# Attention with soft-MoE slots: the order of the V products, a half chunk and a transposition within a pair of heads

## The chip, the cores and the metric

The kernel runs on one core of a Trainium2 chip. The metric is the device time of one execution in microseconds, as the median of several runs. In the profile PE is the matrix engine, PEld its weight loads, DVE the vector engine, ACT the scalar engine, POOL the general engine (it also issues the converting DMAs), SP the engine that issues plain DMAs.

## The reference

Eight images of 12 heads, 448 tokens, 64 channels go through attention whose softmax has one more term exp(-m) in its denominator. The result, as 3584 tokens of 768 channels, goes through a mixture of experts with 32 slots: slots gather tokens by a softmax over all tokens, eight experts of four slots each run two layers, tokens gather slots by a softmax over slots.

```python
scores = scale * np.matmul(q, k.transpose(0, 1, 3, 2))
m = np.max(scores, axis=-1, keepdims=True)
e = np.exp(scores - m)
attn = e / (np.sum(e, axis=-1, keepdims=True) + np.exp(-m) + 1e-09)
x = np.matmul(attn, v)               # then as [3584, 768]
logits = x @ phi                     # [3584, 32]
d = softmax of logits over the tokens;  c = softmax of logits over the slots
slot_input = d.T @ x                 # per expert e: 4 slots
slot_out[e] = np.maximum(slot_input[e] @ w1[e], 0.0) @ w2[e]
out = c @ slot_out
```

## The kernel before

**Pairs.** Heads are worked in 48 pairs (`NPAIR`), six pairs an image, three pairs a group. The 448 query rows of a head are three full chunks of 128 rows and a half chunk of 64; the half chunks of the two heads of a pair share 128 partitions. The loop over `s` is one pair step, its inner loop over `y` two half steps; `hs = 2*s+y`. The order in which the functions are called is the order on each engine (the schedule is written by hand), and an engine works strictly in that order.

**What a pair needs.**
- `T(n)`: 28 transpositions of q and k on PE into one PSUM bank, copied out by ACT (first pair of a group) or DVE (the two others), line 229.
- `A`, `A1`: scores with queries on partitions, only for the row maximum. A full chunk has two (line 268), each with a bank of `psA` and a DVE reduce of 0.6 us (line 270); the half chunk has one bank for both heads (lines 256, 259). They run some four pairs ahead, handed out from the list `runs`.
- `W1`, `W2`, `W3`: once a group, the maxima are negated (POOL), turned (PE) and copied (ACT), and exp(-m) is made (ACT).
- `AB(n, i)`: chunk i of pair n: scores with keys on partitions, minus the maximum by a second matmul (lines 354, 358), then ACT's exponential (line 360); around them the two maximum scores of a pair further on. `Bk(n, 3, 1)` is the half chunk.
- `AV(n, i, qs)`: V products from the exponentials, four key chunks i, into the one bank of `psV`; a column of ones in V gives the denominators. 24 matmuls of full query chunks and 8 of the half chunk (line 393).
- `N1`: the bank is copied to `ubuf` (ACT). `N2`: the denominators (two small DVE operations, lines 414 and 415) and the multiplications (three on POOL, lines 419 to 424).
- `PX(n)`: the pair's result is turned on PE (line 445) and copied to `xT` by ACT (line 451).
- `P(b)`: once an image, six steps for the MoE part, each hung to a half step in `post`: `l_mm` (logits, line 471), `l_turn`, `s_max`, `exps`, `s_mm` (slot inputs, line 539), `c_turn`. Each takes one `psA` bank, except `exps`.

**Banks.** `psA` has 3 (maximum scores, T, the chunk steps), `psB` 4 (scores, W2, PX), `psV` 1.

**Order of a pair step on PE before.** y=0: chunk 0, chunk 1, V products of the pair before (key chunks 2 and 3), a chunk step, their half-chunk products, N1. y=1: chunk 2, half chunk, T for pair s+6, W2, V products of this pair (key chunks 0 and 1), a chunk step, PX of pair s-2, N2.

**Weights and the end.** The first layer's weights and part of the second's are loaded by POOL's converting DMAs into `W` (11 places) during the pairs. Columns of the second layer of experts 4 to 7 come late into `R`, the place of the pairs' own tiles: the first half directly (`load_first`, by `col_at`), the second by way of `wd` in DRAM and SP's queue (`load_second`). After the last pair: `last` (the last image's steps), `hidden` (first layer, line 748), `slots` (second layer, line 764), `pick`, and the outputs, sent by SP as they are made.

Of the kernel before, what the change touches and what calls it, by code (L numbers as in the profile page):

```python
# [8 lines left out]
F32 = mybir.dt.float32  # L9
# [15 lines left out]
HG = 6  # L25
# [6 lines left out]
def kernel(  # L32
# [38 lines left out]
    ident2 = const.tile([128, 128], BF16, name="ident2")  # L71
# [7 lines left out]
    NQK, NE, VPN, NATV = 7, 5, HG * 4 * VS, HG * 4 * D  # L79
    sizes = [("nq0", 2 * NP * S), ("nq1", 2 * NP * S), ("nv", NATV), ("qk6", 2 * S), ("wm1", 512),  # L80
             ("qk0", 2 * S), ("qk1", 2 * S), ("qk2", 2 * S), ("wm0", 512), ("qk3", 2 * S), ("vp0", VPN),
             ("qk4", 2 * S), ("x0", 4 * DD), ("qk5", 2 * S), ("e2", NE * 2 * S), ("e1", S), ("vp1", VPN),
             ("xT", KC * 512), ("x1", 4 * DD)]
# [8 lines left out]
    e1_t = part("e1", 0, S)  # L92
# [3 lines left out]
    xT = part("xT", 0, KC * 512).rearrange("p (j s) -> p j s", j=KC)  # L96
# [23 lines left out]
    W = keep.tile([128, 11 * KC * F], BF16, name="W")  # L120
    w_tile = lambda i: W[:, i * KC * F:(i + 1) * KC * F]
# [10 lines left out]

    dram = ctx.enter_context(tc.tile_pool(name="dram", bufs=1, space=bass.MemoryType.DRAM))
    wd = [dram.tile([128, E2, ND], BF16, name=f"wd{z}") for z in range(FK)]

# [7 lines left out]
    with ExitStack() as at:  # L143
# [8 lines left out]
        ubuf = pu.tile([128, 2, 7 * W65], F32, name="ubuf")  # L152
# [27 lines left out]
        for h in range(2):  # L180
            nc.vector.tensor_add(ident2[:, 64 * h:64 * h + 64], ident[:, 0:64], ident[:, 64:128])
# [22 lines left out]
        mx, ngm, ec, mT, eT, av, us = {}, {}, {}, {}, {}, {}, {}  # L204
# [9 lines left out]
        def T(n):  # L214
            g, pl = divmod(n, NP)
            ps = psA.tile([128, 2, S], BF16, tag="a", name="ps_t")
# [20 lines left out]
        def A(n, i):  # L237
# [4 lines left out]
            if i < 3:  # L242
# [5 lines left out]
                for hl in range(2):  # L248
                    c = HG * i + 2 * pl + hl
                    nc.vector.reduce_max(mx[g][:, c:c + 1], pss[hl][:, 0:S], axis=AX.X)  # L250
            else:
# [6 lines left out]
                c = 3 * HG + pl  # L258
                nc.vector.reduce_max(mx[g][:, c:c + 1], ps[:, 0:S], axis=AX.X)  # L259

        def A1(n, i, hl):
# [7 lines left out]
            c = HG * i + 2 * pl + hl  # L269
# [3 lines left out]
        def W1(g):  # L273
# [4 lines left out]
            cols = lambda t: t[:, 0:3 * HG].rearrange("p (i c) -> p i c", i=3)[:, :, 2 * l0:2 * l1]  # L278
            o = w[:, 0:3, :].rearrange("p i (d c) -> p i d c", d=2)[:, :, :, 2 * l0:2 * l1]
            neg(o, cols(m).unsqueeze(2).to_broadcast([128, 3, 2, 2 * (l1 - l0)]))  # L280
            for hl in range(2):
                r = slice(64 - 64 * hl, 128 - 64 * hl)
                o = w[r, 3, :].rearrange("p (d c) -> p d c", d=2)[:, :, 2 * l0 + hl:2 * l1:2]
                neg(o, m[r, 3 * HG + l0:3 * HG + l1].unsqueeze(1).to_broadcast([64, 2, l1 - l0]))
            if l1 - l0 == NP:
                neg(nm, m)
            else:
                nc.gpsimd.memset(nm, 0.0)
                neg(cols(nm), cols(m))
                neg(nm[:, 3 * HG + l0:3 * HG + l1], m[:, 3 * HG + l0:3 * HG + l1])  # L290
            ngm[g] = nm

        def W2(g):
# [4 lines left out]
            nc.tensor.matmul(ps[:, 384:448], w[:, 3, :], ident2[:, 0:64], start=True, stop=True)  # L298
            st["ps_m"] = ps

        def W3(g):
# [3 lines left out]
            e = psm.tile([128, NP, 7], F32, tag="ec", name="ec", bufs=3)  # L305
            nc.scalar.activation(e[:, :, 0:6].rearrange("p l (i h) -> p i l h", i=3),
                                 ngm[g][:, 0:18].rearrange("p (i l h) -> p i l h", i=3, h=2),
                                 AF.Exp, scale=scale)
            nc.scalar.activation(e[:, :, 6], ngm[g][:, 18:21], AF.Exp, scale=scale)
            ec[g] = e  # L310


        def Bk(n, i, c=0):
# [11 lines left out]
            else:  # L325
# [3 lines left out]
                es = [e1_t]  # L329
# [69 lines left out]
        def N1(n):  # L399
# [4 lines left out]
            u = ubuf[:, n % 2, :].rearrange("p (s c) -> p s c", c=W65)  # L404
# [3 lines left out]
        def N2(n):  # L408
            g, pl = divmod(n, NP)
            b, pb = divmod(n, PB)  # L410
            u = us[n]
            eng = nc.gpsimd if on_pool(n) else nc.vector
# [474 lines left out]
```

## Time and profile before

| | |
|---|---|
| median of 3 runs | 312.85 us (311.38 to 315.28) |
| the profiled execution | 310.7 us, its span 308.9 us |
| PE, DVE, ACT, POOL busy, share of the span | 89%, 83%, 81%, 66% |
| pair steps 5 to 41 | 49.60 to 233.43 us |
| six pairs (186.14 to 216.00) | 29.86 us; DVE and ACT busy 28.56 and 28.57 |
| the first output transfer issued, the last landed | 278.8 us, 307.7 us |

A row of a group has the line, the engine, the operation, its tiles as out<-in with shapes and the count; then busy time and mean length of one in ns; then the engine's idle time just before, and what ended it. A row of the timeline has the start and the length in us, engine and line; a bracket gives the idle time before it and who ended that. A row of the windows has busy time and count for each engine, the granted clock of PE, and the DMA engines' share.

### The profile page before, as it was taken

The page shows a single profiled execution, that of the slowest core. Times are in us where ns is not written, and L with a number is a line of the kernel's source. Part 1 is how long each engine was busy: PE and PEld are TensorE (multiplying, and loading weights), DVE is VectorE, ACT ScalarE, POOL GpSimd, SP SyncE. Part 2 cuts the span into 40 slices and gives each one's busy share as a digit, 9 for nine tenths or more (in the row PEclk, how much of TensorE's full clock was granted, in tenths as well). Part 3 has the DMA queues.
Part 4 walks back from the last instruction along what each step waited for, and adds up shares of the span by engine and source line. Part 5 has one row for each costly group of instructions (what it writes and reads, how often), then busy time and mean ns, then how long its engine had stood idle before and what let it go on. Part 6 is the DMA issues. An engine that isn't in the chain of part 4 may idle for free.

```text
span 308.9 us, 12205 instructions
## 1 busy us (share of the span) xinstructions
PE 275.6 (89%) x5067; PEld 159.0 (51%) x5068; DVE 257.2 (83%) x607; ACT 249.3 (81%) x549; POOL 202.7 (66%) x403
## 2 busy tenths in 40 slices
PE   2899999999999999999999999999999899994810
PEld 1434456565666656665566566656665556451200
DVE  4778999999999999999999999999999566536930
ACT  2357599999999999999999999999999997236810
POOL 8682769788788878896889788879584863000000
PEclk9999999999999999999999999999999999999555
DMA  6999499999999999999999999999971999937997
GB/s 88 149 128 202 64 205 150 198 182 205 163 196 157 210 169 198 155 203 149 149 164 186 177 186 169 196 177 203 166 110 17 144 126 204 337 128 260 415 439 312
DMA packets 49350, 57.44 MB, mean 186 GB/s; under 512 B 2832, under 2 KB 41488, under 8 KB 48912
## 3 DMA queue, kind: packets, MB, share of 16 engines
q0 software_dynamic: 45536, 42.52, 90.1%
q1 hardware_dynamic: 3760, 14.16, 11.5%
q8 instruction: 39, 0.64, 0.8%
q14 instruction: 15, 0.12, 0.1%
HBM read 88.18 MB, written 14.16 MB: 331 GB/s over the span
## 4 chain that ended last, share of the span: by engine, by line
PE 50%; DVE 30%; ACT 7%; issue 4%; POOL 4%; DMA 1%; DVEq 0%; POOLq 0%
DVE mx L270 15%; PE ps_av L393 11%; PE ps_a L268 6%; PE ps_t L224 6%; PE ps_b L354 5%; PE ps_b L358 4%; DVE mx L250 3%; DVE mx L259 3%; PE ps_b L332 3%; PE ps_a L246 2%; DVE W L801 2%; DVE R L229 2%; PE ps_x L445 2%; ACT R L227 2%; PE ps_so L764 2%
## 5 line engine op out<-in xcount | busy, mean ns | idle before, releaser
L270 DVE TENSOR_REDUCE mx<-ps_a 128x1 f32<-128x448 f32 x248 | 136.6, 613 | 5.3 <-PE ps_a L268 5.1
L360 ACT ACTIVATE R<-ps_b 128x448 bf16<-128x448 f32 x272 | 131.0, 573 | 1.1 <-PE ps_b L358 0.8
L268 PE MATMUL ps_a<-R 64*128 64x448 bf16 x248 | 80.5, 352 | 1.8 <-DVE mx L270 1.8
L354 PE MATMUL ps_b<-R 64*128 64x448 bf16 x272 | 73.9, 353 | 0.9
L358 PE MATMUL ps_b<-mT,sel 64*128 64x448 bf16 x272 | 70.6, 350 | 0.0
L393 PEld LDWEIGHTS <-R 128*128 128x128 bf16 (+1 forms) x1536 | 50.5, 101 | 30.5 <-issue 26.4
L393 PE MATMUL ps_av<-R 128*128 128x65 bf16 (+1 forms) x1536 | 64.9, 196 | 0.1
L419 POOL TENSOR_TENSOR R<-ubuf,rec 128x384 bf16<-128x384 f32 x44 | 36.3, 825 | 37.9 <-DVE rec L415 23.4
L224 PEld LDWEIGHTS <-R 64*64 64x64 bf16 x1344 | 31.1, 113 | 19.2 <-issue 7.8
L338 ACT ACTIVATE R<-ps_b 128x448 bf16<-128x448 f32 x64 | 36.0, 579 | 5.9 <-PE ps_b L335 5.9
L224 PE MATMUL ps_t<-ident,R 64*64 64x64 bf16 x1344 | 32.0, 198 | 5.9 <-DMA R<-in_q_dram 4.3
L451 ACT CAST R<-ps_x 128x512 bf16<-128x512 f32 x47 | 28.1, 598 | 5.7 <-PE ps_x L445 5.7
L259 DVE TENSOR_REDUCE mx<-ps_a 128x1 f32<-128x448 f32 x48 | 29.6, 616 | 0.6 <-PE ps_a L256 0.3
L358 PEld LDWEIGHTS <-sel 64*128 64x128 bf16 x272 | 21.5, 94 | 14.9 <-issue 5.3
L268 PEld LDWEIGHTS <-R 64*128 64x128 bf16 x248 | 23.1, 94 | 9.8
L405 ACT COPY ubuf<-ps_av 128x455 f32<-128x455 f32 x44 | 25.2, 573 | 3.0 <-PE ps_av L393 2.8
L227 ACT COPY R<-ps_t 128x896 bf16<-128x896 bf16 x20 | 18.4, 922 | 11.3 <-PE ps_t L224 11.0
L250 DVE TENSOR_REDUCE mx<-ps_a 128x1 f32<-128x448 f32 x40 | 22.6, 618 | 4.3 <-PE ps_a L246 3.9
L332 PE MATMUL ps_b<-R 64*64 64x448 bf16 (+1 forms) x112 | 22.7, 386 | 0.0
L335 PE MATMUL ps_b<-mT,sel 64*64 64x448 bf16 (+1 forms) x112 | 21.5, 366 | 0.0
L424 POOL TENSOR_TENSOR R<-ubuf,rec 128x128 bf16<-128x128 f32 x44 | 17.5, 398 | 3.7
L354 PEld LDWEIGHTS <-R 64*128 64x128 bf16 x272 | 17.2, 94 | 4.7 <-issue 0.2
(132 smaller groups left out, 454.0 us busy)
## 6 DMA issues: line engine op xcount, KB each, us to landing
W<-in_moe_w_dram POOLq DMA_DIRECT2D x22, 768.0 KB, 9.5
R<-in_v_dram POOLq DMA_DIRECT2D x32, 192.0 KB, 4.6
out_dram<-W SPq DMA_DIRECT2D x2, 2688.0 KB, 10.3
R<-in_q_dram POOLq DMA_DIRECT2D x15, 336.0 KB, 7.4
R<-in_k_dram POOLq DMA_DIRECT2D x15, 336.0 KB, 8.5
wd<-in_moe_w_dram POOLq DMA_DIRECT2D x8, 384.0 KB, 10.0
R<-wd SPq DMA_DIRECT2D x8, 384.0 KB, 8.6
R<-in_moe_w_dram POOLq DMA_DIRECT2D x2, 768.0 KB, 8.3
```

The costliest lines, as they stand in the source:

```text
L224: nc.tensor.transpose(ps[r, a, c:c + 64], src[r, pl, tok * D:(tok + 1) * D], ident[r, r])
L250: nc.vector.reduce_max(mx[g][:, c:c + 1], pss[hl][:, 0:S], axis=AX.X)
L259: nc.vector.reduce_max(mx[g][:, c:c + 1], ps[:, 0:S], axis=AX.X)
L268: nc.tensor.matmul(ps[:, 0:S], t[r, 0, i * 128:(i + 1) * 128], t[r, 1, :], start=True, stop=True)
L270: nc.vector.reduce_max(mx[g][:, c:c + 1], ps[:, 0:S], axis=AX.X)
L332: nc.tensor.matmul(outs[hl], t[rs[hl], 1, cols], t[rs[hl], 0, :], start=True, stop=False)
L338: nc.scalar.activation(e, p[:, 0:S], AF.Exp, scale=scale)
L354: nc.tensor.matmul(ps[hl][:, 0:S], t[rs[hl], 1, cols], t[rs[hl], 0, :], start=True, stop=False)
L358: nc.tensor.matmul(ps[hl][:, 0:S], sel[rs[hl], h:h + 1].to_broadcast([64, 128]), mT[mg(n)][rs[hl], :], start=False, stop=True)
L360: nc.scalar.activation(e[:, hl, :], ps[hl][:, 0:S], AF.Exp, scale=scale)
L393: nc.tensor.matmul(o, eT[n, i, hl][:, qc], vp[g % 2][:, 2 * pl + hl, i, 0:W65], start=(i == 0 and u == 0 and hl == 0), stop=(i == 3), skip ...
L419: eng.tensor_mul(x[:, 0:3, c:c + 128].rearrange("p i (h d) -> p i h d", h=2), u[:, 0:6, 0:D].rearrange("p (i h) d -> p i h d", h=2), rec[: ...
```

## The change

- A pair step now is: y=0: chunk 0, half chunk, T for pair s+6. y=1: chunk 1, chunk 2, W2, the chunk step, PX of pair s-4, then all 32 V products of pair s-1, then N1. The list `runs` has the half chunk second, to match. The last four pair steps keep the old order; `px_at` hands out the PX left over.
- From pair 8 on, T writes to the bank of `psV` instead of one of `psA`.
- `N2` takes two pairs at once in every second pair step: one set of denominators (14 columns) and one small multiplication for both. The maxima's columns are sorted by pair for it, exp(-m) is one ACT operation and lives in one ring `ecr`; `ubuf` has four places for two, `e2` six for five, `e1` two for one.
- The chunk steps stand at odd half steps, one in each pair step, from `12*b + 21` on.
- `xT` has 448 columns an image slice for 512: PX turns the half chunk into 64 columns, `l_mm` takes it as two matmuls of 64 rows, `t_mm` reads it twice.
- The last two small operations of `c_turn` are done once for all images at the end.
- `W` is half a place smaller. The second half of expert 2's second layer goes to DRAM early (`w2d`) and by SP's queue into the place of expert 3's first layer once `hidden(0)` has read it. The first columns of expert 7 go to DRAM at s = 37 (`w3d`) and come by SP's queue, ahead of `load_second`.

```diff
-    NQK, NE, VPN, NATV = 7, 5, HG * 4 * VS, HG * 4 * D
+    NQK, NE, VPN, NATV = 7, 6, HG * 4 * VS, HG * 4 * D
...
-    W = keep.tile([128, 11 * KC * F], BF16, name="W")
+    NW = 21 * KC * F // 2
+    W = keep.tile([128, NW], BF16, name="W")
...
-        ubuf = pu.tile([128, 2, 7 * W65], F32, name="ubuf")
+        ubuf = pu.tile([128, 4, 7 * W65], F32, name="ubuf")
...
         def T(n):
             g, pl = divmod(n, NP)
-            ps = psA.tile([128, 2, S], BF16, tag="a", name="ps_t")
+            ps = (psA if n < 8 else psV).tile([128, 2, S], BF16, tag="a" if n < 8 else "v", name="ps_t")
...
-        def N2(n):
...
-            rec = psm.tile([128, 7], F32, tag="rec", name="rec", bufs=3)
-            nc.vector.scalar_tensor_tensor(rec, u[:, :, D], 1e-9, ec[mg(n)][:, pl, :], op0=ALU.add, op1=ALU.add)
+        def N2(*ns):
+            k, n0 = len(ns), ns[0]
...
+            nc.vector.scalar_tensor_tensor(rec, den, 1e-9, ecr[:, 7 * (n0 % 6):7 * (n0 % 6 + k)], op0=ALU.add, op1=ALU.add)
             nc.vector.reciprocal(rec, rec)
...
-                    for i in range(4):
+                    for i in range(3):
                         nc.tensor.matmul(v["ps_l"][:, i, :], xT[:, j, i * 128:(i + 1) * 128], phi_sb[:, j, :],
                                          start=(j == 0 and i == 0), stop=(j == KC - 1), skip_group_check=True)
+                for j in js:
+                    for r in (slice(0, 64), slice(64, 128)):
+                        nc.tensor.matmul(v["ps_l"][r, 3, :], xT[:, j, 384:S], phi_sb[:, j, :],
+                                         start=False, stop=(j == KC - 1), skip_group_check=True)
...
-                nc.vector.tensor_scalar(r, r, 1e-9, None, op0=ALU.add)
-                nc.vector.reciprocal(r, r)
...
-                post[2 * (PB * b + PB + 2) + z + (z > 2) + (z > 4) if b < B - 2 else 2 * (PB * b + PB + 2) - 1 + z] = f
+                hs = 2 * (PB * b + PB + 4) + 1
+                post[hs + 2 * z - (max(z - 2, 0) if b == B - 3 else 0) if b < B - 2 else hs - 3 + z] = f
...
-        runs = [(n, i) for n in range(NPAIR) for i in range(4)]
+        runs = [(n, i) for n in range(NPAIR) for i in (0, 3, 1, 2)]
...
+        px_at = {88: (40,), 89: (41,), 92: (42,), 93: (43, 44), 95: (45,)}
...
-                elif s < NPAIR:
+                elif s == 2 or s >= NPAIR - 4:
                     AB(s, 2 * y)
...
+                elif y == 0:
+                    AB(s, 0)
+                    Bk(s, 3, 1)
+                    if s < NPAIR - 6:
+                        T(s + 6)
+                else:
+                    AB(s, 1)
+                    AB(s, 2)
...
+                    elif s % 2 and s >= 3:
+                        N2(s - 3, s - 2)
...
+                if hs in post:
+                    post[hs]()
...
+                if y and not tail:
+                    if s < NPAIR - 5 and s >= 4:
+                        PX(s - 4)
+                    if s:
+                        for i in range(4):
+                            AV(s - 1, i, range(3))
+                        for i in range(4):
+                            AV(s - 1, i, [3])
+                        N1(s - 1)
...
         AV(n, 3, range(4))
+        nc.sync.dma_start(out=late[0][:, 3, :, :], in_=w3d)
         load_second(0, 4)
...
         hidden(0, h0, range(2))
+        nc.sync.dma_start(out=w_two, in_=w2d)
         last[3]()
+        nc.vector.tensor_scalar(crec, crec, 1e-9, None, op0=ALU.add)
+        nc.vector.reciprocal(crec, crec)
```

## The prediction

> **What bounds the kernel now.** I read the page first, then the busy times of one six-pair round, then the groups by line, then the timeline of a pair, last the end of the kernel.
>
> ```profile
> span 308.9 us, 12205 instructions
> PE 275.6 (89%) x5067; PEld 159.0 (51%) x5068; DVE 257.2 (83%) x607; ACT 249.3 (81%) x549; POOL 202.7 (66%) x403
> ...
> PEclk9999999999999999999999999999999999999555
> ```
>
> ```profile
> core 0: us, PE busy (x) PEld busy (x) DVE busy (x) ACT busy (x) POOL busy (x), PEclk, DMA share, GB/s
> 186.14:216.00 29.86, 29.35 (x593) 18.24 (x591) 28.56 (x68) 28.57 (x65) 25.45 (x50) 1.00 1.18 186
> ```
>
> ```profile
> L270 DVE TENSOR_REDUCE mx<-ps_a 128x1 f32<-128x448 f32 x248 | 136.6, 613 | 5.3 <-PE ps_a L268 5.1
> ...
> L229 DVE COPY R<-ps_t 128x896 bf16<-128x896 bf16 x28 | 17.2, 615 | 0.0
> ```
>
> The page has PE, DVE and ACT near each other and the clock full until the last three slices. The window 186.14 to 216.00 is six pairs (one round: the work repeats every six, 12 heads making one image), 4.98 us a pair. DVE and ACT are both busy 28.56 of 29.86 us. PE's 29.35 is no demand: a matmul row lasts 0.35 us though the next starts 0.19 us later, so short waits hide in it. The timeline of one pair shows them.
>
> ```profile
> 204.54 3.23 DVE L270 TENSOR_REDUCE mx<-ps_a 128x1 f32<-128x448 f32 x6
> 205.17 0.35 PE L268 MATMUL ps_a<-R 64*128 64x448 bf16 x1 [0.30 <-DVE mx L270]
> 205.45 0.79 PE L393 MATMUL ps_av<-R 128*128 128x65 bf16 x20
> 206.17 0.36 PE L268 MATMUL ps_a<-R 64*128 64x448 bf16 x1
> ...
> 206.56 0.35 PE L268 MATMUL ps_a<-R 64*128 64x448 bf16 x1
> 206.84 0.38 PE L332 MATMUL ps_b<-R 64*64 64x448 bf16 x2
> ...
> 207.29 0.63 PE L224 MATMUL ps_t<-ident,R 64*64 64x64 bf16 x28
> ...
> 207.85 0.54 PE L393 MATMUL ps_av<-R 128*128 128x65 bf16 x12
> ...
> 208.23 0.39 PE L445 MATMUL ps_x<-ident,R 128*128 128x128 bf16 x4
> ...
> 208.55 0.36 PE L268 MATMUL ps_a<-R 64*128 64x448 bf16 x1
> ...
> 208.95 0.62 DVE L270 TENSOR_REDUCE mx<-ps_a 128x1 f32<-128x448 f32 x1 [0.33 <-PE ps_a L268]
> ```
>
> Six reduces take 3.23 us: one each 0.53. PE's score matmul at 205.17 waited for the first of them (ended near 205.11): a `psA` bank is free again 0.06 us after its reduce. An idle DVE starts 0.40 us after the matmul (208.55, 208.95). So the loop is: PE fills three `psA` banks, DVE empties them at 0.53 us, and PE may be away from scores only as long as these banks feed DVE. Now the V products are away for 0.7 us (20 of them) and 0.4 us (12), and DVE hardly idles: 1.3 us per round. PE's own starts, added up without these waits, make some 28.4 us a round, so DVE sets the pace, with PE close behind.
>
> **The change, steady pairs (s = 5 to 41).** They run from 49.60 (first score of pair step 5) to 233.43, 183.8 us.
>
> Savings by rows: the two denominator operations take 0.31 us from start to start (L414, L415), once for two pairs: 0.15 a pair off DVE. `c_turn` loses L548 and L549, 0.3 a round. One mode change of PE less a pair, 0.1. ACT: one of two exponentials of 0.2 us in three pairs, and 64 of 512 columns of a 598 ns copy (0.05 to 0.07). DVE's demand falls from 28.56 to about 27.4 a round. That is the whole gain on offer, 1.2 a round.
>
> The price is the order. After the change PE does in a pair: chunk 0, half chunk, T, chunk 1, chunk 2, PX, all 32 V products. DVE does: two reduces, half chunk's reduce, T's copy, (every second pair) the denominators, then the four reduces of chunks 1 and 2. Intervals by the rows above: chunk's first to second score 0.39, into the half chunk 0.28, to T 0.45, T and mode change 0.56, chunks 1 and 2 0.97 (0.39+0.19+0.39). The last score is thus due at 2.65 us. Its bank is the one of chunk 1's first score, three allocations earlier, so it also needs DVE at: 0.40 + 3 x 0.53 + 0.58 + 0.06 = 2.63; plus 0.53 where DVE copies T (two pairs of three); plus 0.30 with denominators. From that last score to the next pair's first: 0.28 into PX, 0.19 for PX, 0.72 for the first 20 V products and 0.37 for 12 more, 1.56 us (plus 0.21 where W2 stands there, each third pair). At its start DVE has three reduces left, 1.5 us of work, and gets the next 1.56+0.40 later: half a microsecond idle in every pair, which is new.
>
> Pairs by s modulo 6, without chunk steps of the MoE part: 0: 2.65+1.56 = 4.21; 1: 5.04; 2: 4.95; 3: 4.51; 4: 4.74; 5: 5.25. Sum 28.7.
>
> The chunk steps (`P(b)`) now all stand between the last score and PX, where PE alone sets the time; before, they lay in PE's slack. A step's own `psA` tile waits for chunk 1's second reduce, about 0.55 after the last score where PE is there at 0.28 (with W2 at 0.49). So: l_mm 0.27 + 0.88 (18 full matmuls at 0.025, 12 halves, two mode changes of 0.1); l_turn 0.06 + 0.2; s_max 0.27 + 0.06; s_mm 0.06 + 0.7 (28 at 0.025); c_turn 0.27 + 0.06. Together 2.8 a round; their DVE work is hidden there. 28.7 + 2.8 = 31.5 a round, 5.25 a pair, against 29.9 now. Over 37 pairs: six rounds 189.0, the last pair 5.5 (with its l_turn), less 1.7 for steps 5 to 9, where no image is complete yet: 192.8 against 183.8, **+9.0 us**. Bounds: if the steps' matmuls found cover (28.7 a round) it would be -6; if the half microsecond were idle on top of today's 1.3 a round, +17.
>
> No cost taken: T into `psV` needs the copy N1 of the block before (ACT, done about 0.65 into the pair; T is due at 1.12), and the V block needs T's copy (at 2.6 by DVE, 2.8 by ACT; due at 3.1). If that cover of 0.3 to 0.5 were gone it would cost about 0.5 a pair. POOL's two pairs of multiplications (L419, 825 ns, and L424) come once for two pairs; PX is a pair later than that, some 5 us of cover. What queues behind them on POOL are the loads, none of them due sooner than two pairs. A fourth `ubuf`, a sixth `e2`, and the earlier T on loaded q and k: nothing waits.
>
> **The change, from s = 42 on.** s = 42 and 43 take 4.5 and 5.8 against 4.46 and 5.03: +0.8 (s_mm and 12 V products more in s = 43). The last four pairs go by ACT (4.00 of 4.00 busy from 244 to 248), and get two more PX copies (0.45 each) and l_ev: **+1.1** (0 to 2). Then the new transfer `w_two`:
>
> ```profile
> 258.92 7.67 SPq L141 DMA_DIRECT2D R<-wd  x8
> ...
> 268.75 1.48 PE L748 MATMUL ps_h<-W,ubuf 128*32 128x512 bf16 x24
> ...
> 272.44 0.34 PE L764 MATMUL ps_so<-W 128*32 128x384 bf16 x3
> ```
>
> ```profile
> out_dram<-W SPq DMA_DIRECT2D x2, 768.0 KB, 4.3
> ```
>
> It may start when hidden(0) has read its place, about 268.6 (before the row at 268.75), stands on SP's queue behind nine other transfers, and is wanted half way through the slots that start at 272.44, at 273.1. A transfer of 768 KB took 4.3 us, so 272.9 at best plus issue; behind the others, whose last landed at 274.7 now (some 2 us sooner, as 768 KB of converting loads leave the busy stretch), 274 to 276. I take **+1** (0 to 3): the output transfers start only after it, so all of it reaches the end. The two operations on `crec` moved here lie under 7 us of matmuls: 0. Of DMA rings the Trainium skill says that descriptors are consumed in ring order on each engine (DMA: Bandwidth & Descriptors, Queues, rings and completion order); by it `w_two` gets nothing before the nine, near the middle of that range, and by the 4.3 us row alone it would cost 0.
>
> Sum: 9.0 + 0.8 + 1.1 + 1 = +11.9. The profiled execution took 310.7 us (308.9 span), so 322.6; the median shown is 312.85, 2.15 above it, so 324.75, and I say **324**. A measurement of this kernel tells about 2% from no change: 306.6 to 319.1.
>
> **Rivals.**
> - Faster: the three-bank ring never runs dry, because T's tile has left `psA` (eight tiles a pair before, seven now). Then DVE works without idling: 27.4 a round, -2.5 x 6.2 = -15, +2.9 after: 300.6. It decides from the point where PE's way from last to first score falls under DVE's remaining 1.5 us less 0.4. For it: DVE is near saturated today, and a block costs one mode change less. Against: 1.56 is longer than 1.1, by rows. 0.13.
> - No change: half of the steps' matmuls and half of the idle time find cover; a round stays near 30: 313 to 317. For it: a PE wait hidden in 0.35 us rows can be shorter than I think. 0.18.
> - Worse: the one `psV` bank passes between T, its copy, the block and N1, and one of the four is late each time by 0.5: 37 x 0.5 more, 342. Against: cover above. 0.06.
> - Much worse: PE's clock. PE will stand up to 0.8 us in most pairs; should the granted clock fall to the 0.5 that the page shows in its last three slices (from 286 us), the streamed part (some 3.7 us a pair) doubles and a pair takes about 8.5: 37 x 3.3, near 430. The trace speaks against it: the wait at 205.17 is of this kind and PEclk is 1.00 in the whole round. 0.01. The Trainium skill describes such a failure, micro-idle gaps between matmul groups that let the clock oscillate (TensorE: Matmul & The Clock Gate, A second HAM failure mode); this trace has not shown it.
>
> **How the numbers follow.** Forecast (318 to 331) 0.62; no change 0.18; faster 0.13; worse or much worse 0.07. Range: the forecast's own with the upper half of the rivals below it, 309 to 332. Faster 0.13, same 0.18, slower 0.69.
>
> **What would show it.** Right: in a pair after the change, DVE idle about 0.5 us before the first reduce, ended by PE's first score; PE waiting 0.5 to 0.8 us before the last score, ended by DVE's reduce; a round of 31 to 32 us; DVE's busy time in it near 27.4; PEclk 1.00. PE idle before the second half of the first slots, ended by the DMA of `w2d`. Wrong: a round under 30 us, DVE busy above 95%, or T waiting for ACT's N1.

## The result and the profile after

The changed kernel took 327.47 us (median of 4 runs, 326.98 to 329.55), the kernel before 312.12 us beside it. The ratio is 1.0486 with a 95% interval of 1.0396 to 1.0576: slower by about 15 us. The forecast was 324 in a range of 309 to 332.

The page of the changed kernel, its first lines and the granted clock:

```profile
span 325.7 us, 12324 instructions
...
PE 274.5 (84%) x5115; PEld 162.3 (50%) x5116; DVE 249.1 (76%) x548; ACT 249.0 (76%) x532; POOL 193.7 (59%) x394
...
PEclk9999999999999999999999999999999999998555
```

Before, PE, DVE and ACT were busy for 89%, 83% and 81% of the span, now for 84%, 76% and 76%. DVE did get less work, 249.1 us against 257.2. But no engine is full any more, and the span is 16.8 us longer. So the added time is waiting. The groups by line say who waits (the last field is the idle time before the row's instructions, and who ended it):

```profile
L289 DVE TENSOR_REDUCE mx<-ps_a 128x1 f32<-128x448 f32 x248 | 137.9, 612 | 25.7 <-PE ps_b L366 10.3
...
L287 PE MATMUL ps_a<-R 64*128 64x448 bf16 x248 | 81.1, 352 | 13.1 <-DVE mx L289 12.1
```

The row of the score matmuls in the kernel before:

```profile
L268 PE MATMUL ps_a<-R 64*128 64x448 bf16 x248 | 80.5, 352 | 1.8 <-DVE mx L270 1.8
```

DVE's reduces waited for 5.3 us before and wait for 25.7 now. PE's score matmuls waited for 1.8 us before and wait for 13.1 now, nearly all of it for DVE. Each of the two engines waits for the other, at different places of the pair. The list of waits gives the count and the longest of one:

```profile
PE ps_a L287 <- DVE mx L289: 12.1, 26, 0.6
...
DVE mx L289 <- PE ps_b L366: 10.3, 14, 1.5
```

All of DVE's 25.7 us stand before the first reduce of a pair, 0.40 or 0.47 us after the pair's first score. (The profile names the instruction that ended last before the reduce could start, so some of these waits stand under line 366, the score matmul next to line 287 on PE.) In the steady pairs s mod 6 = 0 to 5 they are 0.62, 0.34, 0.49, 0.56, 0.38 and 1.05 us long. PE's waits for DVE stand before the last score of a pair in four pairs of six, 0.60, 0.34, 0.28 and 0.65 us for s mod 6 = 1, 2, 4 and 5.

The timeline of one pair (the second of six, step s with s mod 6 = 1, without an image's chunk step of PE) shows both waits in place:

```profile
216.18 0.36 PE L287 MATMUL ps_a<-R 64*128 64x448 bf16 x1
...
216.58 1.16 DVE L289 TENSOR_REDUCE mx<-ps_a 128x1 f32<-128x448 f32 x2 [0.34 <-PE ps_a L287]
...
217.25 0.60 PE L243 MATMUL ps_t<-ident,R 64*64 64x64 bf16 x28
...
218.18 0.61 DVE L248 COPY R<-ps_t 128x896 bf16<-128x896 bf16 x1
...
218.71 0.18 DVE L428 SCALAR_TENSOR_TENSOR rec<-ubuf,ecr 128x14 f32<-128x14 f32 x1
...
218.92 0.24 DVE L429 RECIPROCAL rec<-rec 128x14 f32<-128x14 f32 x1
...
219.08 2.15 DVE L289 TENSOR_REDUCE mx<-ps_a 128x1 f32<-128x448 f32 x4
...
219.69 0.35 PE L287 MATMUL ps_a<-R 64*128 64x448 bf16 x1 [0.60 <-DVE mx L289]
219.97 0.37 PE L463 MATMUL ps_x<-ident,R 128*128 128x128 bf16 x4
```

From the same timeline, the lines that follow:

```profile
221.25 0.36 PE L287 MATMUL ps_a<-R 64*128 64x448 bf16 x1
...
221.72 1.16 DVE L289 TENSOR_REDUCE mx<-ps_a 128x1 f32<-128x448 f32 x2 [0.49 <-PE ps_a L287]
```

PE's last score of the pair (219.69) waited 0.60 us for a `psA` bank, because DVE began the four reduces of chunks 1 and 2 at 219.08 only, behind the copy of T and the denominators. Then PE is away from scores for 1.56 us, until 221.25. DVE runs dry meanwhile and waits 0.49 us for the next pair's first score. The order makes the pair 219.69 − 216.18 + 1.56 = 5.07 us long. One round of six pairs, from the windows:

```profile
190.55:222.19 31.64, 29.17 (x603) 18.61 (x599) 27.72 (x61) 28.57 (x64) 24.22 (x49) 1.00 1.15 179
```

The round takes 31.64 us for 29.86, with DVE busy for 27.72 of it (28.56 before) and the clock of PE at 1.00.

Where the span grew, stage by stage, from the times of the first instruction of each stage in the two traces:

| stage | before | after | difference | forecast |
|---|---|---|---|---|
| start to the first score of step 5 | 49.60 | 48.48 | −1.1 | 0 |
| steps 5 to 41 | 183.8 | 194.7 | +10.9 | +9.0 |
| steps 42 and 43 | 9.49 | 10.96 | +1.5 | +0.8 |
| step 44 to the last image's logits | 17.52 | 19.59 | +2.1 | +1.1 |
| from there to `slots` | 12.01 | 12.03 | 0 | 0 |
| `slots` to the first output transfer | 6.35 | 8.35 | +2.0 | +1 |
| first output issued to last landed | 28.92 | 30.44 | +1.5 | 0 |

The differences add up to 16.9 for 16.8 us of span.

### The profile page after: what moved, and what is told of

Its sections match the earlier page's. It is cut to its first block, busy times and chain, and to the rows that moved or that the text cites. A ratio compares the mean times of both kernels' runs of the same rounds, so it can differ in the third digit from the quotient of the medians.

```text
span 325.7 us, 12324 instructions
## 1 busy us (share of the span) xinstructions
PE 274.5 (84%) x5115; PEld 162.3 (50%) x5116; DVE 249.1 (76%) x548; ACT 249.0 (76%) x532; POOL 193.7 (59%) x394
## 4 chain that ended last, share of the span: by engine, by line
PE 42%; DVE 38%; POOL 6%; issue 4%; DMA 3%; ACT 3%; DVEq 0%; POOLq 0%; ACTq 0%
DVE mx L289 20%; PE ps_av L405 14%; PE ps_a L287 6%; DVE mx L278 6%; DVE R L248 4%; PE ps_x L463 3%; DVE mx L269 3%; DMA W<-w2d 2%; PE ps_o L843 2%; PE ps_t L243 2%; PE ps_b L366 2%; PE ps_s L562 2%; PE ps_so L811 2%; DVE rec L429 1%; PE ps_l L489 1%
## 5 line engine op out<-in xcount | busy, mean ns | idle before, releaser
L289 DVE TENSOR_REDUCE mx<-ps_a 128x1 f32<-128x448 f32 x248 | 137.9, 612 | 25.7 <-PE ps_b L366 10.3
L372 ACT ACTIVATE R<-ps_b 128x448 bf16<-128x448 f32 x272 | 130.1, 565 | 8.3 <-PE ps_b L370 7.5
L287 PE MATMUL ps_a<-R 64*128 64x448 bf16 x248 | 81.1, 352 | 13.1 <-DVE mx L289 12.1
L405 PE MATMUL ps_av<-R 128*128 128x65 bf16 (+1 forms) x1536 | 56.0, 195 | 1.2 <-DVE R L248 0.7
L405 PEld LDWEIGHTS <-R 128*128 128x128 bf16 (+1 forms) x1536 | 48.6, 100 | 7.4 <-issue 4.6
L243 PEld LDWEIGHTS <-R 64*64 64x64 bf16 x1344 | 30.1, 112 | 16.0 <-issue 5.4
L350 ACT ACTIVATE R<-ps_b 128x448 bf16<-128x448 f32 x64 | 34.9, 564 | 4.0 <-PE ps_b L347 3.8
L243 PE MATMUL ps_t<-ident,R 64*64 64x64 bf16 x1344 | 30.6, 195 | 5.5 <-DMA R<-in_q_dram 4.2
L417 ACT COPY ubuf<-ps_av 128x455 f32<-128x455 f32 x44 | 24.5, 557 | 12.1 <-PE ps_av L405 12.0
L370 PEld LDWEIGHTS <-sel 64*128 64x128 bf16 x272 | 24.7, 95 | 13.0 <-issue 2.1
L469 ACT CAST R<-ps_x 128x448 bf16<-128x448 f32 x47 | 26.3, 564 | 2.0 <-PE ps_x L463 1.8
L287 PEld LDWEIGHTS <-R 64*128 64x128 bf16 x248 | 23.2, 94 | 8.2 <-issue 0.9
L246 ACT COPY R<-ps_t 128x896 bf16<-128x896 bf16 x20 | 18.4, 918 | 10.9 <-PE ps_t L243 10.8
L296 POOL TENSOR_SCALAR R<-mx 128x18 bf16<-128x18 f32 (+5 forms) x68 | 16.8, 253 | 12.5 <-DVE mx L269 6.4
L463 PEld LDWEIGHTS <-R 128*128 128x128 bf16 x192 | 12.6, 99 | 12.7 <-issue 11.1
```

The costliest lines, as they stand in the source:

```text
L243: nc.tensor.transpose(ps[r, a, c:c + 64], src[r, pl, tok * D:(tok + 1) * D], ident[r, r])
L287: nc.tensor.matmul(ps[:, 0:S], t[r, 0, i * 128:(i + 1) * 128], t[r, 1, :], start=True, stop=True)
L350: nc.scalar.activation(e, p[:, 0:S], AF.Exp, scale=scale)
L370: nc.tensor.matmul(ps[hl][:, 0:S], sel[rs[hl], h:h + 1].to_broadcast([64, 128]), mT[mg(n)][rs[hl], :], start=False, stop=True)
L372: nc.scalar.activation(e[:, hl, :], ps[hl][:, 0:S], AF.Exp, scale=scale)
L405: nc.tensor.matmul(o, eT[n, i, hl][:, qc], vp[g % 2][:, 2 * pl + hl, i, 0:W65], start=(i == 0 and u == 0 and hl == 0), stop=(i == 3), skip ...
```

## The experiments

The main theory: the order of the pair costs the time, since PE is away from scores longer than three banks feed DVE, and DVE has the copy of T and the denominators ahead of the reduces that PE waits for. The rivals: the one `psV` bank now shared by T; the mode changes of PE (scores run as 64*128, the V products and PX as 128*128; the first matmul of the other form starts 0.28 us after a score, as at 219.97 above, where a further score starts after 0.19) and the new half-chunk forms; the chunk steps that lost their cover; the late second-layer transfer. Ratios are against the kernel before. Plain differences are of medians, against the changed kernel where nothing else is said.

### The new transfer put first in its queue

```diff
-        load_second(4, 8)
...
         nc.sync.dma_start(out=w_two, in_=w2d)
+        load_second(4, 8)
```

> The changed kernel with one edit: the last four transfers of load_second are issued behind w_two instead of ahead of it. Theory (the 2.0 us for which PE stands still in the first slots come from w_two lying behind eight transfers on SP's queue): w_two lands 2 to 3 us earlier, the slots' row shrinks from 3.16 to about 1.2 us, and the whole kernel is 2.0 us shorter (1.5 to 2.3), near 325.4. Rival (the transfer is late because it cannot start before hidden(0) is done): the wait stays above 1.5 us and the time within 0.5 of 327.5.

Measured: 325.62 us, 1.0464 (1.0423 to 1.0505), 1.85 less than the changed kernel. The end of the changed kernel, in its timeline:

```profile
281.38 0.32 SPq L819 DMA_DIRECT2D W<-w2d  x1
...
285.77 0.34 PE L811 MATMUL ps_so<-W 128*32 128x384 bf16 x3
...
288.44 0.32 PE L811 MATMUL ps_so<-W 128*32 128x384 bf16 x1 [1.67 <-DMA W<-w2d]
```

And the row of that transfer in the list of DMA issues (size, time from issue to landing), first of the changed kernel, then of the experiment:

```profile
W<-w2d SPq DMA_DIRECT2D x1, 768.0 KB, 7.0
```

```profile
W<-w2d SPq DMA_DIRECT2D x1, 768.0 KB, 4.3
```

PE stood 1.67 us for the transfer, which took 7.0 us behind the others and takes 4.3 us ahead of them. It was issued at about the same time in both (281.38, 281.62). The `slots` stage is back at 6.35 us. So the two microseconds come from the place in the queue, not from the transfer itself. The Trainium skill says that descriptors are consumed in ring order on each engine (DMA: Bandwidth & Descriptors, Queues, rings and completion order); these two rows agree with it.

### The denominators behind chunk 2

```diff
-                    elif s % 2 and s >= 3:
-                        N2(s - 3, s - 2)
                 else:
+                    if s % 2 and s >= 3 and not tail:
+                        N2(s - 3, s - 2)
```

> The changed kernel with one edit: N2 of two pairs stands behind chunk 2 (where DVE idles during the V products) instead of behind T. Theory (PE's last score waits for the reduce of chunk 1's first score, and whatever DVE does ahead of that reduce lengthens the pair): pair steps 1, 3 and 5 of six lose 0.3 us each, 0.9 a round, 5 to 5.5 us in all, near 322. Rival (DVE's total work or PE's alone sets the pace, the place of two small operations is indifferent): within 1 us of 327.5.

Measured: 324.42 us, 1.0432 (1.0389 to 1.0475), 3.05 less, where 5 to 5.5 less was expected. The three odd pairs of a round (s mod 6 = 1, 3, 5) became 0.31, 0.22 and 0.30 us shorter, as they should. But the pair with s mod 6 = 2 became 0.56 longer (6.32), and a round is only 0.2 us shorter. So steps 5 to 41 have no more than 1.2 of the 3.05 us; 1.1 stand behind the pairs, where the edit changes no order (`slots` to the first output 7.63 for 8.35, the output phase 30.01 for 30.44). The list of waits of this run has a row that was not foreseen:

```profile
PEld L312 <- POOL R L296: 8.6, 8, 1.4
```

Line 312 is `W2` on PE, line 296 `W1` on POOL. `W1` now stands on POOL behind the multiplications of two pairs, which began half a step later.

### The same, with the negated maxima ahead of the multiplications

```diff
-                    if s % 2 and s >= 3 and not tail:
+                    if s % 2 and s >= 3 and s % 3 != 1 and not tail:
                         N2(s - 3, s - 2)
...
                     W1((s + 2) // 3 + 1)
+                if s % 2 and 3 <= s < NPAIR - 4:
+                    N2(s - 3, s - 2)
```

(The added call stands under `if s % 3 == 1`, so that each pair of pairs is still worked once.)

> e2_denoms_late with N2 called behind W1 where both fall into one pair step (s = 1 modulo 6). Theory (in e2_denoms_late W1 stands on POOL behind the multiplications of two pairs, so W2 on PE waits for it, and pair step 2 of six takes 6.32 instead of 5.76 us): that pair goes back to 5.8, 0.5 us a round, about 3 us less than e2_denoms_late, near 321. Rival (W2 waits there for the maxima from DVE): no change, 324.4.

Measured: 321.43 us, 1.0338 (1.0299 to 1.0378), 3.0 less than the run before it and 6.0 less than the changed kernel. The pair is back at 5.76 us, the round at 30.9, which is 0.75 less than in the changed kernel, or 4.6 us over 37 pairs; the rest of the 6.0 lies outside them. The wait of PE for DVE went from 12.1 to 8.1 us, its longest from 0.6 to 0.3:

```profile
PE ps_a L287 <- DVE mx L289: 8.1, 26, 0.3
```

So DVE's two small operations ahead of the reduces cost 0.2 to 0.3 us in each second pair. They cost it because PE waited for exactly those reduces.

### T in a `psA` bank again, and the V products in two blocks

```diff
-            ps = (psA if n < 8 else psV).tile([128, 2, S], BF16, tag="a" if n < 8 else "v", name="ps_t")
+            ps = psA.tile([128, 2, S], BF16, tag="a", name="ps_t")
```

> The changed kernel with one edit: T writes to psA for all pairs, as before the change, and psV serves the V products alone. Theory (the psV bank is free in time, the loss is in the order): within 1.5 us of 327.5. Rival (T, its copy, the V block and N1 wait for each other at the one bank): 4 us or more faster.

Measured: 327.89 us, 1.0543 (1.0492 to 1.0595), 0.4 more than the changed kernel, with a round of 31.9. A bank of its own for the V products brings nothing. The run alone does not price the sharing, since T now takes a `psA` bank; the row of the V products in the changed kernel does:

```profile
L405 PE MATMUL ps_av<-R 128*128 128x65 bf16 (+1 forms) x1536 | 56.0, 195 | 1.2 <-DVE R L248 0.7
```

PE's rows show 1.2 us of idle time ahead of them in the whole kernel, 0.7 of it for the copy of T.

With T in `psA`, 12 of the 24 full V products (those of key chunks 0 and 1) go between chunk 1 and chunk 2:

```diff
                     AB(s, 1)
+                    if s > 2:
+                        for i in (0, 1):
+                            AV(s - 1, i, range(3))
                     AB(s, 2)
...
-                        for i in range(4):
+                        for i in (0, 1, 2, 3) if s <= 2 else (2, 3):
                             AV(s - 1, i, range(3))
```

> The edit of e3_t_own_bank, and the V products in two blocks again: 12 of them (key chunks 0 and 1) between chunk 1 and chunk 2, the other 20 at the end as now. Everything else as in the changed kernel. Theory (a stretch without scores that is longer than what three psA banks hold starves DVE): the stretch shrinks by 0.37 us, the 12 products lie in PE's wait where DVE copies T or makes denominators; four or five pairs of six gain 0.35, 1.4 to 1.8 a round, so 8 to 11 us less, 316 to 320. Rival (mode changes of PE are what counts, and one block has fewer): two mode changes more a pair, 0.2 us, some 8 us more, 335.

Measured: 317.98 us, 1.0211 (1.0166 to 1.0256), 9.5 us less than the changed kernel and 9.9 less than the run with T in `psA`. The six pairs at their usual lengths add up to 30.3 us; the complete rounds of the trace took 30.0 to 31.1. The rows that answer to the two waits:

```profile
L289 DVE TENSOR_REDUCE mx<-ps_a 128x1 f32<-128x448 f32 x248 | 138.6, 612 | 15.6 <-PE ps_a L287 6.9
...
L287 PE MATMUL ps_a<-R 64*128 64x448 bf16 x248 | 87.6, 353 | 0.4 <-DVE mx L269 0.2
```

PE's wait for DVE is gone (0.4 for 13.1) and DVE's idle time went from 25.7 to 15.6. Twelve matmuls in another place, no work less: this is the largest single part of the loss. Of the 9.9 us, 8.6 stand in steps 5 to 41 (196.4 and 187.8 us).

### One block, done alone to the kernel before

The converse, in the kernel before, with none of the other changes. All full V products of the pair before stand in one block between chunk 1 and chunk 2:

```diff
                     if 0 <= s - 1:
-                        for i in (2, 3):
+                        for i in range(4):
                             AV(s - 1, i, range(3))
...
-                    if s < NPAIR:
+                    if s == NPAIR - 1:
                         for i in (0, 1):
                             AV(s, i, range(3))
```

> The kernel before the change with one edit: all V products of the pair before stand in one block between chunk 1 and chunk 2 (24, then the chunk step, then 8) instead of 12 there and 12 at the end of the pair step; everything else as before the change. Theory (a stretch without scores longer than three banks feed DVE costs its excess in each pair): the stretch grows from 1.0 to 1.45 us, DVE idles 0.3 to 0.4 in the four pairs of six in which it sets the pace, a round grows from 29.9 to 31 to 32, the kernel is 8 to 13 us slower, 320 to 325. Rival (mode changes of PE are what counts): one less a pair, 0.1 us, 3 to 4 us faster, 308.

Measured: 321.25 us, 1.0348 (1.0291 to 1.0405), 10.2 more than the kernel before (311.07 in that comparison). A round of it, and the row of the reduces:

```profile
163.50:195.15 31.65, 30.47 (x595) 18.08 (x593) 28.77 (x69) 28.61 (x66) 24.68 (x48) 1.00 1.05 163
```

```profile
L270 DVE TENSOR_REDUCE mx<-ps_a 128x1 f32<-128x448 f32 x248 | 138.7, 613 | 13.5 <-PE ps_a L268 13.4
```

The round is as long as that of the changed kernel, without its new half-chunk forms, turned order or shared bank. One mode change less does not make up for it. DVE waits 13.5 us for PE's scores where it waited 5.3.

### A fourth bank for the maxima

```diff
-        psA = pool("psA", 3, space=PSUM)
-        psB = pool("psB", 4, space=PSUM)
+        psA = pool("psA", 4, space=PSUM)
+        psB = pool("psB", 3, space=PSUM)
```

> The changed kernel with one edit: psA has 4 banks and psB 3 (before: 3 and 4). Theory (three psA banks are too few for a stretch of 1.56 us without scores): PE's waits for DVE before the last score nearly vanish and DVE is no longer idle before a pair's first reduce; what the pair then takes depends on ACT's three banks, where chunk 2's second score would wait for chunk 1's first exponential (some 0.3 to 0.6 us a pair): a round of 28.5 to 31, the kernel 312 to 324. Rival (the wait for DVE is no matter of banks): waits for DVE as now, and the loss of a psB bank on top, 330 or more.

Measured: 328.35 us, 1.0556 (1.0501 to 1.0611): no gain, where 312 to 324 was expected. The wait only changed its place. The rows of its list of waits:

```profile
DVE mx L289 <- PE ps_a L287: 23.9, 41, 1.1
PE ps_b L366 <- ACT R L372: 20.6, 45, 0.8
```

PE no longer waits for DVE to free `psA`, but now 45 times for ACT to free one of only three `psB` banks, 20.6 us in all. DVE still waits 23.9 us for scores, which the theory had taken away. The run shows that `psB` needs its four banks in this order. It cannot show what a fourth `psA` bank is worth, since the bank had to come from somewhere: on that it is inconclusive.

### The chunk steps behind T

```diff
-                post[hs + 2 * z - (max(z - 2, 0) if b == B - 3 else 0) if b < B - 2 else hs - 3 + z] = f
+                post[hs - (b < B - 3) + 2 * z - (max(z - 2, 0) if b == B - 3 else 0) if b < B - 2 else hs - 3 + z] = f
```

> The changed kernel with one edit: the steps of the MoE part (P(b), images 0 to 4) stand half a pair step earlier, behind T instead of behind chunk 2. Theory (behind chunk 2 their matmuls are exposed in full and wait 0.27 for a psA bank; behind T they lie in PE's wait, but their DVE work comes ahead of chunk 1's reduces): l_mm's pair loses 0.6 to 0.8, the others change by -0.1 to +0.2, so 0.3 to 0.7 a round, 2 to 4 us less, 323.5 to 325.5. Rival (the steps cost their matmuls' time wherever they stand): within 1 us of 327.5.

Measured: 325.04 us, 1.0455 (1.0384 to 1.0526), 2.4 less. The pair with `l_mm` went from 5.84 to 5.29 us, and the round from 31.63 to 31.18. So part of the chunk steps' time does depend on where they stand. The run whose trace this is took 327.77, longer than its other three (323.43 to 325.18): one pair in it (s = 28) took 8.20 us, and the figures here are of rounds without it.

### The old order with the change's savings

The changed kernel with the pair order of before (half chunk behind chunk 2, V products in two blocks at the old places, T in `psA`, chunk steps at the old half steps but one pair later, as PX is), and with the denominators of two pairs, the narrower `xT`, the one exponential, the late `crec` and the new transfers kept:

```diff
-        runs = [(n, i) for n in range(NPAIR) for i in (0, 3, 1, 2)]
+        runs = [(n, i) for n in range(NPAIR) for i in range(4)]
...
+                    for i in (0, 1):
+                        AV(s, i, range(3))
...
+                if y and not tail and s >= 3:
+                    PX(s - 3)
...
+                if y and s and s % 2 == 0 and on_pool(s - 1):
                     N2(s - 2, s - 1)
```

> The changed kernel with the order of a pair step taken back to the one before the change (chunks 0 and 1, V products in three pieces, chunk 2, half chunk, T in psA, a chunk step at any half step), everything else kept: denominators of two pairs at once, one exponential, 448 columns, the two operations of c_turn at the end, the three new transfers; PX one pair later than before the change, since its multiplications come for two pairs. Theory (the loss is in the order, the savings are real where DVE sets the pace): a round of 28.6 to 29.3 us (29.9 before the change, less some 1 us of DVE's work), 16 to 18 us less than the changed kernel, 309 to 312. Rival (the savings bring nothing, as PE sets the pace in the old order): a round as before the change, 29.9, and with the new transfers and the longer end 315 to 317.

Measured: 316.38 us, 1.0158 (1.0086 to 1.023). The order alone gives back 11 us. But the complete rounds are 30.1 to 30.9 us (29.9 to 30.6 before the change), not under 29.3: the savings are not seen. The pair with s mod 6 = 5 takes 6.02 us. It now has `s_mm`, whose pair took 5.16 before. Its timeline:

```profile
170.10 0.83 POOL L435 TENSOR_TENSOR R<-ubuf,rec 128x384 bf16<-128x384 f32 x1
...
170.89 0.41 POOL L442 TENSOR_TENSOR R<-ubuf,rec 128x128 bf16<-128x128 f32 x1
...
171.27 1.16 POOL L296 TENSOR_SCALAR R<-mx 128x18 bf16<-128x18 f32 x4
...
172.39 0.28 POOL L296 TENSOR_SCALAR ngm<-mx 128x21 bf16<-128x21 f32 x1
...
172.48 0.20 PE L313 MATMUL ps_m<-ident,R 128*128 128x64 bf16 x1 [0.31 <-POOL R L296]
```

Two pairs' multiplications fill POOL, and `W1` (line 296) comes behind them, so `W2` on PE waits. It is the wait of the second experiment, at another place.

The same with the new transfer first in its queue:

```diff
-        load_second(4, 8)
...
         nc.sync.dma_start(out=w_two, in_=w2d)
+        load_second(4, 8)
```

> e6_old_order with the edit of e1_wtwo_first. Both theories: 1.5 to 2 us less than e6_old_order. If the savings are real it is at 307 to 310, faster than both kernels.

Measured: 315.89 us, 1.0154 (1.0103 to 1.0206), only 0.5 us less than without, which lies within the spread of the runs (315.24 to 316.87 here). `slots` to the first output took 7.23 us there and 6.34 here, so there was less to win than in the new order.

### The two orders, each with all the repairs

The old order of the last run, with `W1` ahead of the multiplications where they meet, and with 512 columns of `xT` an image and the logits' matmuls as before:

```diff
-                if y and s and s % 2 == 0 and on_pool(s - 1):
+                if y and s and s % 2 == 0 and s % 3 != 1 and on_pool(s - 1):
                     N2(s - 2, s - 1)
...
                     W1((s + 2) // 3 + 1)
+                if s % 2 == 0 and on_pool(s - 1):
+                    N2(s - 2, s - 1)
...
-             ("xT", KC * S), ("x1", 4 * DD)]
+             ("xT", KC * 512), ("x1", 4 * DD)]
...
-                    for i in range(3):
+                    for i in range(4):
```

> e7_old_order_wtwo with N2 behind W1 where both fall into one pair step (s = 4 modulo 6), and xT, PX, l_mm and t_mm as before the change (512 columns, l_mm of 24 whole matmuls), which has 96 instructions less on PE. Theory: W2's wait for POOL goes (0.5 a round, 3 us), and the 16 KB packet of the instruction queue that lies in the output phase of all kernels since the change falls elsewhere, which gives back the 1.1 us by which that phase is longer than 28.9: 311 to 313, level with the kernel before. Rivals: the round stays at 30.1 (W2's wait is not POOL's), and the output phase at 30.0 though no such packet lies in it.

Measured: 310.43 us over 10 runs, 0.9965 (0.9933 to 0.9998). The last two rounds in its trace are 29.53 and 29.54 us (the three ahead of them 29.8 to 30.3), its output phase is 28.89.

The new order with T in `psA`, the V products in two blocks, the denominators behind chunk 2, `W1` first, the transfer first, and `xT` and logits as before:

```diff
                     AB(s, 1)
+                    if s > 2:
+                        for i in (0, 1):
+                            AV(s - 1, i, range(3))
                     AB(s, 2)
...
+                    if s % 2 and s >= 3 and s % 3 != 1 and not tail:
+                        N2(s - 3, s - 2)
...
-        load_second(4, 8)
...
         nc.sync.dma_start(out=w_two, in_=w2d)
+        load_second(4, 8)
```

> The changed kernel with all edits that helped, in its own order of chunks: V products in two blocks and T in psA (e4_v_split), w_two ahead of the second half of load_second (e1_wtwo_first), N2 behind chunk 2 and behind W1 (e9_w1_first), l_mm and xT as before the change. Theory: 318.0 less 1.9, less 3 to 5 for N2, less 1.5 to 3 for l_mm and the output phase: 307 to 311.5, at or under the kernel before (311.6). Rival (in the split order DVE's place no longer matters, PE's starts alone set the pair): N2's edit brings nothing, 313 to 315.

Measured: 309.02 us over 10 runs (308.77 to 310.59), 0.9947 (0.9923 to 0.9972): the fastest of all, half a per cent under the kernel before. A round of it, in the window of its trace:

```profile
155.03:184.49 29.46, 29.36 (x598) 18.18 (x593) 27.96 (x61) 28.35 (x64) 23.52 (x48) 1.00 1.08 174
```

Four of the repairs were also run singly or by steps: two blocks −9.5, denominators and `W1` −6.0, the transfer −1.85. Together they make −17.4 of the −18.45 us between the changed kernel and this one. These are medians of several chips, on which the kernel before took 311.07 to 312.12 us, so the remaining microsecond is within what they can tell. The parts also overlap: the output phase alone gave back 1.55 (30.44 to 28.89), on which more below, and the run with two blocks already had `slots` to the first output at 7.25 us for 8.35.

Against the kernel before, stage by stage, this last kernel wins 2.1 us ahead of step 5 and 2.6 in steps 5 to 41 (181.2 for 183.8), and loses 0.6 in steps 42 and 43 and 2.6 from step 44 to the last image's logits (20.12 for 17.52). That last loss came with the change, and no run was aimed at it.

## Why the prediction was right, and where its sizes were off

**The mechanism, right.** PE's way of 1.56 us from the last score to the next first one, DVE dry for half a microsecond behind it, and PE waiting 0.5 to 0.8 before the last score were all foretold. The timeline has 1.56, 0.49 and 0.60. Over all pairs DVE's idle time is 0.34 to 1.05 us; PE's wait reaches the forecast size in two pairs of six, is shorter in two, and the rows show none in the other two. The split of the block took the loss away, and the one block alone made it in the kernel before. The forecast of the round was 31.5 us; it was 31.64. Pair by pair, for s mod 6 = 0 to 5, the forecast with each pair's chunk step added:

| | 0 | 1 | 2 | 3 | 4 | 5 |
|---|---|---|---|---|---|---|
| forecast | 4.54 | 5.04 | 5.71 | 4.84 | 5.89 | 5.51 |
| measured | 4.60 | 5.07 | 5.76 | 4.82 | 5.84 | 5.54 |

**The steady pairs, +9.0 forecast, +10.9 measured.** Of the 1.9, steps 5 to 9 have 0.64: they were taken 1.7 shorter than steady ones, since no image was complete, and were less so. One pair (s = 20) took 6.33 where 5.71 was due, another 0.6: there `W2` on PE waited for `W1` on POOL, as shown below. The rest is 0.13 a round. Against that, the first steps ended 1.1 us sooner, which was not in the sum at all.

**Steps 42 and 43, +0.8 forecast, +1.5 measured.** Step 43 took 6.43 for 5.8. Its last 12 V products started at 253.70, 0.5 us behind PX, since ACT was still copying the block before out of `psV`. The sum did not have this wait: it took the hand-over of that one bank as covered, and here, where two blocks follow each other, it is not.

**The last four pairs, +1.1 forecast (0 to 2), +2.1 measured.** The bound was passed by a little. The step that failed is "The last four pairs go by ACT". ACT's busy time rose by 0.57 (16.33 to 16.90 us), less than the 1.1 that was added for it, while its idle time rose by 1.5. In the changed kernel ACT's exponentials waited four times for PE's scores there, 2.3 us in all (0.5 before), the longest 0.88 us, behind `s_mm` and `c_turn` on PE. So PE held ACT up where ACT was taken to set the pace. No run moved these steps, so the price of each stays open.

**The second-layer transfer, +1 forecast (0 to 3), +2.0 measured.** The mechanism and the order in the queue were right, and shown by the run with the transfer first. The transfer landed at 288.39, 2.6 us after `slots` began; the forecast's 274 to 276, counted from `slots` at 272.44, is 1.6 to 3.6 us. So the landing lay in the middle of what was forecast, and the +1 taken from it was the low end. The queue ahead was done 1.5 us sooner and not 2 (0.76 us after `slots` began for 2.27).

**The output, 0 forecast, +1.5 measured.** This step failed outright: the part behind `slots` was taken as unchanged. See below.

**The sum, +11.9 forecast, 16.8 us of span measured.** The four stages that were priced and the output all came out longer than forecast, and only the start came out shorter. The wide range took this in, and the sum itself was too low.

**The costs taken as nothing.** T in `psV`: right in the steady pairs, where taking it out again gained nothing, and wrong once, in step 43. POOL: right but for one pair, and its reason was incomplete. "What queues behind them on POOL are the loads" left out `W1`, which is on POOL too. In the changed kernel this cost 0.6 us at s = 20, where POOL issued one more transfer (to `wd`, 0.82 us at 125.44) ahead of the multiplications, as its timeline shows:

```profile
125.44 0.82 POOL L156 DMA_DIRECT2D wd<-in_moe_w_dram  x1
...
127.73 0.83 POOL L435 TENSOR_TENSOR R<-ubuf,rec 128x384 bf16<-128x384 f32 x1
...
128.90 1.16 POOL L296 TENSOR_SCALAR R<-mx 128x18 bf16<-128x18 f32 x4
...
130.11 0.20 PE L313 MATMUL ps_m<-ident,R 128*128 128x64 bf16 x1 [0.30 <-POOL R L296]
```

With `W1` ahead of the multiplications this pair took 5.76 us like the others. The cover was so thin that moving the denominators half a step later cost 0.56 us in each pair with s mod 6 = 2, and the old order with doubled multiplications 0.57 us in its own (6.02, and 5.45 with `W1` first). Two of the runs above fell short of their expectation by it.

**The gain on offer, 1.2 us a round.** DVE's busy time fell by 0.84 (28.56 to 27.72), not by 1.2. And even the two repaired kernels, where DVE is relieved and the order costs little, run a round in 29.53 and 29.46 against 29.86 in the kernel before. Only 0.3 to 0.4 arrive. In the window of the new order PE is busy for 29.36 of 29.46 us, DVE for 27.96. The waits in that window say the same: no row of PE waits for another engine, while DVE waits 1.4 us and ACT 0.8 us for PE. PE's starts stand close behind DVE's, as the prediction said of the kernel before, so relieving DVE uncovers PE.

**The rivals.** Faster (the ring never runs dry): the idle row of 25.7 us is against it. No change: it rested on the chunk steps finding cover. The pairs came out as forecast with the steps' full time in them, so behind chunk 2 they had next to none; behind T they had some. Worse by the shared bank: the run with T in `psA` gained nothing, and PE's idle 1.2 us ahead of the V products are far from the 37 times 0.5 of this rival. The clock: PE waited 26 times for up to 0.6 us and PEclk stayed 1.00 in all rounds shown. The rule in the Trainium skill about micro-idle gaps between matmul groups (TensorE: Matmul & The Clock Gate, A second HAM failure mode: psum-queue depth-cycling) did not come true in this trace.

## What to carry to other kernels

Where a producer feeds a consumer through a ring of banks, write down the producer's longest stretch without producing, and compare it with what the ring holds: here three banks of 0.53 us against 1.56 + 0.40 us. Joining two short blocks into one long one saves a mode change, and lengthens that stretch; moving 12 matmuls back was worth 9.5 of 15 us. And before an operation is batched on an engine that runs in strict order, look at everything that queues behind it there, not only at who waits for its result.

## What was not expected of the hardware

The outputs are the same transfers in both kernels, yet the phase took 30.44 us for 28.92. The DMA queues of the output phase, with packets, megabytes and share of the 16 engines' time, and one size of transfer with its median time; first of the kernel before (278.7 us to the end), then of the changed one (295 us to the end):

```profile
q1 hardware_dynamic: 2608, 11.01, 90.3%
...
out_dram<-W SPq DMA_DIRECT2D x2, 576.0 KB, 3.7
```

```profile
q1 hardware_dynamic: 2608, 11.01, 88.9%
q8 instruction: 1, 0.02, 0.3%
...
out_dram<-W SPq DMA_DIRECT2D x2, 576.0 KB, 4.7
```

The changed kernel has one packet of 16 KB of instructions in the phase, on queue 8, which kept one DMA engine for 1.41 us, from 7.65 to 9.06 us after the first output was issued. The first five output transfers land as in the kernel before (the fifth at 7.97 us after the first issue, for 7.86), and the sixth and all later ones land late (11.35 for 9.48). The likely reason is that the output's share on that engine comes later by as much as the packet took, and a transfer has not landed without it. The same packet lies in the output phase of all ten kernels here that have the half-chunk logits matmuls (12324 instructions in the changed one, 12205 before). Their phase is 0.88 to 1.51 us longer than 28.92, with packets of 0.93 to 1.41 us. (Six of the ten, the changed one among them, also have an 8 KB packet on queue 14 at the start of the phase; the other four do without it and are 0.88 to 1.12 us longer.) The kernel before and the three others (the one block alone and the two with the logits as before) have none in the phase, and 28.89 to 28.92 us. The old order with all repairs was expected to lose it with those matmuls, and did. So packet and delay go together in 14 kernels; neither was tried by itself, and what decides where the packet falls stays open.
